# Key sums with stationary values, filled-up matmuls, split first loads and a new stage order in a gated linear-attention and GEGLU kernel

## The chip, the cores and the metric

The kernel runs on one core of one Trainium2 chip. The metric is the device time of one execution of the whole program, in microseconds; of several runs the median counts. On a core five engines work side by side, each through its own queue, in the order in which the program hands it instructions: TensorE (PE, with PEld for its weight loads), VectorE (DVE), ScalarE (ACT), GpSimd (POOL) and SyncE (SP). SP, ACT and POOL also issue DMAs.

## The reference

A block of linear attention and a gated MLP are mixed token by token (S = 2048 tokens, D = 576, 32 heads of 18, DF = 4608):

```
q, k, v = split(x @ wqkv)                      # 32 heads of 18
phi(t)  = where(t > 0, t + 1, exp(t)) + 1e-6
kv  = sum over tokens of phi(k) x v            # per head, 18 x 18
z   = sum over tokens of phi(k)
o   = (phi(q) @ kv) / (phi(q) . z + 1e-6)
a   = o @ wo
b   = (gelu(x @ w_gate) * (x @ w_up)) @ w_down
out = g * a + (1 - g) * b,    g = sigmoid(sum(x * gate_w))
```

## The kernel before

All matmul operands are float32 held as a high and a low part (fp32r tiles with "hi" and "lo"), and a product is taken as hi·hi + hi·lo + lo·hi. `split` makes the parts: ACT copies the high part, DVE (or POOL) subtracts it for the low one. D = 576 is cut into two halves of 128 + 128 + 32 rows; the three 32-row pieces of a half (hi·hi, hi·lo, lo·hi) share one matmul of 96 partitions, so a projection is 14 matmuls.

The program runs through four stages.

**Start and prologue.** `x0` and `raw_of` are the first input tiles and the K|V weights `wkv`, loaded on SP's queue in column and row pieces; `x_split` and `w_part` split them into `xo` (inputs) and `kvw[i]`, i the half. `proj_mm(t, c, ...)` projects token tile t (128 tokens) onto the column part c of `CH` (378, 326 and 450 columns: keys; the rest of the keys, the first values and the gate; the values). The first two token tiles are held open in six PSUM tiles, four of pool `bank` and two of pool `pair`, and their 84 matmuls are handed out by the operands' order of arrival.

**Key stage.** For each of 16 token tiles the projection, then `kv_post` (phi of the keys into `pkh` and `pkl`, values into `vt`), then `kv_state`, two tiles behind: for five groups of heads (126, four times, and 72 columns) it adds phi(k) transposed times [1 1 | v hi | v lo] to PSUM (`acc_a`, `acc_b`), the keys stationary and `vt` moving, once with `pkh` and once with `pkl`. Behind the projections run loads and splits for later stages.

**Mixing stage.** Its order is written out by hand in word lists given to `run(...)`; a word is a letter and hexadecimal arguments, and each word hands its instructions to the engines' queues at once. For a batch b of 512 tokens, a group g of heads, a token tile t of the batch or a third kt of the rows:

- `s` sums out of PSUM (and masked per head), `t` transposes them, `u` splits them, `z` stores the row of key sums to `z_d` and reads it back, `n` makes the den weights `zmk`, `v` the gates
- `w i o f l c`: load of wo, its split, the product `head_out` of a group's kv with wo, its store to `kw_d`, the load of `kwr` in rows of 128 and its split into `KW`
- `Q a h d`: query projection (14 matmuls of 512 columns; 10 for group 4), phi of it into `r`, its split into `hl`, the `den` matmuls
- `r`: reciprocals. The denominators of 32 heads are copied out by ACT, added and inverted by DVE, stored to `rden_d` repeated per row, and read back as `rb` with 128 partitions
- `p m e`: r times `rb`, split (`p`); the mixed product with `KW` (28 matmuls of 288 columns into one `pair`); its scaled copy by ACT and store (`ga`)
- `x` (`keep_x`): three stores of 1280 KB each of `xo` slots that the MLP's second half needs
- `X y Y`: load of a chunk of inputs in another arrangement (`xc`), its sums and differences on DVE, its split by ACT and POOL into the slots S1 to S4 of `xo`
- `W G g`: first weights and first products of the MLP

PSUM holds here three `bank` tiles, two `pair` tiles (of two banks each) and one `den`. `hl` has three buffers, `p` two, `rb` three; `r` of batch 1 takes the tile of batch 2's.

**MLP.** A Strassen-like scheme of seven products a feature block, over 18 blocks, twice; its order is the table `ORDER`.

Of the kernel before, what the change touches and what calls it, by code (L numbers as in the profile page):

```python
# [8 lines left out]
F32 = mybir.dt.float32  # L9
# [18 lines left out]
CW = 126 + NG * 64 + 128  # L28
# [22 lines left out]
def tile_gated_mix(ctx, tc, xt, xs, wkv, wq, wo, wgu, wgt, wdn, cst, out):  # L51
# [8 lines left out]
    rden_d = {(b, h): dram.tile([H, DH, BS // 2], F32, name=f"rden_d{b}{h}") for b in range(NB) for h in range(2)}  # L60
# [95 lines left out]

    KTS = [(i, kt) for i in range(2) for kt in range(3)]
# [22 lines left out]
    CH = [(0, 378), (378, 326), (704, 450)]  # L180
# [46 lines left out]
    def kv_state(t):
        _, ph, pl = pk.pop(t)
        v = vt.pop(t)
        for g in range(NG):  # L230
            w = 2 + 2 * GR[g]
            mv = v[:, g * VW:g * VW + w]
            if g < 4:
                o = acc_a[:GR[g], g // 2, (g % 2) * VW:(g % 2) * VW + w]
            else:
                o = acc_b[:GR[g], 0, :w]
            for i, p in enumerate((ph, pl)):
                nc.tensor.matmul(o, p[:, GO[g]:GO[g] + GR[g]], mv,  # L238
                                 start=(t == 0 and i == 0 and g in (0, 2, 4)),
                                 stop=(t == NST - 1 and i == 1), skip_group_check=True)  # L240
# [3 lines left out]
    for n, (t, c) in enumerate(first):  # L244
        ps_of[t, c] = bank() if n < 4 else pair()[:, 0]
# [155 lines left out]
    rs = [rp.tile([128, NG, BS], F32, name=f"r{i}") for i in range(3)]  # L401
    r_of = {2: rs[0], 3: rs[1], 0: rs[2], 1: rs[0]}
# [63 lines left out]
    wide = acc_a[:126, :, :2 * VW].rearrange("p a (b c) -> p a b c", b=2)  # L466
    last = acc_b[:72, 0]

    def sums_out():
        nc.vector.tensor_copy(zc[:126, :4].rearrange("p (a b) -> p a b", a=2), wide[:, :, :, 0])  # L470
        nc.vector.tensor_copy(zc[:72, 4:5], last[:, 0:1])
# [6 lines left out]
        nc.sync.dma_start(zq[:, :4], at(0, [[1, 128], [128, 4]]))  # L478
        nc.sync.dma_start(zq[:, 4:5], at(512, [[0, 2], [1, 64], [1, 1]]))

    def states_out():
        four = (lambda v: v[:126, :4].rearrange("p (a b) c -> p a b c", a=2))
        low = tp.tile([128, D], F32, name="low")
        kvl, kvl_last = low[:, :504].rearrange("p (g c) -> p g c", g=4), low[:72, 504:]
        nc.scalar.activation(four(kvl), wide[:, :, :, 128:254], AF.Copy)
        nc.scalar.activation(kvl_last, last[:, 74:146], AF.Copy)
        nc.vector.tensor_tensor(four(kvm), wide[:, :, :, 2:128], four(kvl), OP.add)
        nc.vector.tensor_tensor(kvm[:72, 4, :72], last[:, 2:74], kvl_last, OP.add)

        for g in range(NG):  # L490
            R = GR[g]
            nc.vector.tensor_tensor(kvm[:R, g, :R], kvm[:R, g, :R], mask[:R, :R], OP.mult)

    turned = []

    def states_turn():
        tps = pair()
        turned[:] = [tps[:GR[g], g // 4, (g % 4) * 126:(g % 4) * 126 + GR[g]] for g in range(NG)]
        for g in range(NG):
            R = GR[g]  # L500
            nc.tensor.transpose(turned[g], kvm[:R, g, :R], ident[:R, :R])
# [27 lines left out]
    def head_out(g):  # L529
# [3 lines left out]
        kh, kl = kvt[:R, g, 0, :R], kvt[:R, g, 1, :R]  # L533
# [64 lines left out]
    def reciprocals(b):  # L598
        ps = den_of.pop(b)
        for h in range(2):  # L600
# [6 lines left out]
            nc.sync.dma_start(src, bass.AP(tensor=rd.tensor, offset=rd.offset, ap=[list(rd.ap[0]), [0, DH], [1, HB]]))  # L607
        for h in range(2):
            src, rb = rden_d[b, h], rb_of[b, h]
            nc.sync.dma_start(rb[:, :4], bass.AP(  # L610
                tensor=src.tensor, offset=src.offset, ap=[[HB, 128], [128 * HB, 4], [1, HB]]))
            nc.sync.dma_start(rb[:, 4], bass.AP(
                tensor=src.tensor, offset=src.offset + 512 * HB, ap=[[0, 2], [HB, 64], [1, HB]]))
# [12 lines left out]
    def mixed(b, t):  # L626
# [3 lines left out]
        ops += [(p[:, 0, 4], KW[:, 0, 4]), (p[:64, 0, 4], KW[:64, 1, 4])]  # L630
# [45 lines left out]
h11 e31 p32 d10 d11 Y1 p33 m32 h12 d12 a13 e32 p01 m33 W0 h13 h14 e33 p00 X2 y2 d13 m01 d14 r1 m00 Y2  # L676
# [57 lines left out]
G1 G6 G7 g1 p03 G2 e01 m03 p02 g6 e00 g7 e03 m02 p10 m10 e02 p11 m11 W1 p13 e10 p12 e11 g2 m13 e13 m12 e12  # L734
# [356 lines left out]
```

## Time and profile before

| what | value |
|---|---|
| three runs | 1532.23, 1524.12, 1527.63 us; median 1527.63 |
| profiled execution | 1529.19 us; its span from first to last instruction 1527.4; mean granted clock 0.998 |
| busy share of the span | PE 99%, PEld 87%, DVE 72%, POOL 49%, ACT 38% |
| DMA | 293.57 MB in 117884 packets, mean 192 GB/s |
| prologue's matmuls end | 24.24 us |
| key stage's last matmul ends | 146.6 us |
| mixing stage's last mixed product ends | 306.3 us |

The span is shorter than the execution's time because the program's entry and exit lie around it. Busy shares are averages over the whole span; the MLP from 306 us on makes up four fifths of it, so they say little on the stages in front of it, which the change touches. Those are read by stretches.

### The profile page before, as it was taken

The numbers are of one execution on the slowest core, as the hardware profiler recorded it, in microseconds if no ns is written. First come the engines' busy times: TensorE is split into PE (matmuls) and PEld (weight loads), VectorE is DVE, ScalarE is ACT, GpSimd is POOL, SyncE is SP. The second block draws the span as 40 slices with busy tenths as digits, with TensorE's granted clock in tenths as the row PEclk, the third lists the DMA queues.
The fourth block names the chain that finished last, engine by engine and source line by source line (L and its number), as shares of the span: only waits on it lengthen the run. The fifth ranks groups of instructions, "written<-read, shape, count | busy, mean of one in ns | idle before, by whom it ended". The sixth has DMA issues, their size and how long they took to land.

```text
span 1527.4 us, 21407 instructions
## 1 busy us (share of the span) xinstructions
PE 1505.2 (99%) x8179; PEld 1326.5 (87%) x8179; DVE 1106.8 (72%) x1693; ACT 578.8 (38%) x967; POOL 745.2 (49%) x710
## 2 busy tenths in 40 slices
PE   8999999999999999999999999999999999999998
PEld 8999778788888888888888888888888888888887
DVE  6444567578888888888887777777777777777776
ACT  6555655334334333343434323223222222232223
POOL 1474222167878788788776724323233223232323
PEclk9999999999999999999999999999999999999999
DMA  5676666655665667656556475433443344334441
GB/s 202 201 257 224 204 170 218 211 190 200 220 226 205 226 241 261 235 204 222 201 193 225 143 303 206 179 146 137 175 173 136 136 158 175 137 145 184 181 173 62
DMA packets 117884, 293.57 MB, mean 192 GB/s; under 512 B 6806, under 2 KB 88918, under 8 KB 107414
## 3 DMA queue, kind: packets, MB, share of 16 engines
q1 hardware_dynamic: 114258, 279.48, 52.1%
q10 hardware_dynamic: 3236, 10.63, 1.9%
q0 software_dynamic: 288, 2.10, 0.4%
q8 instruction: 64, 1.05, 0.3%
q14 instruction: 38, 0.31, 0.1%
HBM read 177.15 MB, written 115.03 MB: 191 GB/s over the span
## 4 chain that ended last, share of the span: by engine, by line
PE 92%; DMA 3%; POOL 2%; issue 2%; ACT 1%; DVE 1%; SPq 0%; POOLq 0%; DVEq 0%; ACTq 0%
PE bank L694 52%; PE pair L791 25%; PE bank L187 8%; PE pair L633 3%; PE bank L421 1%; PE pair L238 1%; DMA raw<-wo 1%; POOL xo L660 1%; DMA xo<-xop_d 1%; DMA xc<-xs 1%; POOL sums L781 0%; POOL kw L557 0%; PE pair L187 0%; PE pair L993 0%; DMA raw<-wkv 0%
## 5 line engine op out<-in xcount | busy, mean ns | idle before, releaser
L713 DVE TENSOR_TENSOR sums<-pair,sums 128x576 f32<-128x576 f32 x474 | 354.6, 754 | 160.9 <-PE pair L791 149.0
L694 PE MATMUL bank<-xo,wg 128*128 128x512 f32 x1764 | 442.0, 393 | 5.1 <-POOL xo L660 2.4
L694 PE MATMUL bank<-xo,wu 128*128 128x512 f32 x1764 | 430.4, 393 | 0.8 <-DVE p L713 0.8
L694 PEld LDWEIGHTS bank<-xo,wu 128*128 128x128 f32 x1764 | 323.8, 188 | 64.3 <-DVE p L713 1.2
L694 PEld LDWEIGHTS bank<-xo,wg 128*128 128x128 f32 x1764 | 322.5, 188 | 65.6 <-POOL xo L660 3.6
L791 PEld LDWEIGHTS pair<-wd,h 128*128 128x128 f32 x1680 | 248.2, 189 | 17.3
L791 PE MATMUL pair<-wd,h 128*128 128x288 f32 x1680 | 259.2, 296 | 0.0
L791 PEld LDWEIGHTS pair<-wd,hx 128*128 128x128 f32 x1260 | 179.1, 189 | 9.3
L791 PE MATMUL pair<-wd,hx 128*128 128x288 f32 x1260 | 184.4, 295 | 0.0
L707 ACT ACTIVATE p<-bank 128x512 f32<-128x512 f32 x72 | 43.0, 597 | 354.5 <-PE bank L694 348.3
L857 POOL TENSOR_TENSOR wd<-draw,wd 128x432 fp32r<-128x432 f32 x68 | 75.1, 1123 | 191.8 <-ACT wd L707 191.8
L833 POOL TENSOR_TENSOR h<-e,h 128x512 fp32r<-128x512 f32 x70 | 96.4, 1377 | 140.6 <-ACT h L707 140.6
L833 POOL TENSOR_TENSOR hx<-e,hx 128x512 fp32r<-128x512 f32 x70 | 96.6, 1401 | 112.7 <-ACT hx L707 112.7
L707 ACT ACTIVATE h<-e 128x512 fp32r<-128x512 f32 x107 | 67.3, 629 | 211.9 <-DVE e L713 211.9
L849 POOL TENSOR_TENSOR work<-work 128x256 f32<-128x256 f32 x136 | 113.4, 844 | 6.0 <-DMA work<-wgu 0.6
L187 PE MATMUL bank<-kvw,xo 128*128 128x378 f32 (+5 forms) x560 | 106.9, 345 | 5.8 <-ACT kvw L81 5.7
L187 PEld LDWEIGHTS bank<-kvw,xo 128*128 128x128 f32 (+1 forms) x560 | 97.3, 192 | 10.3 <-ACT kvw L81 6.2
L713 DVE TENSOR_TENSOR u<-bank,p 128x512 f32<-128x512 f32 x72 | 49.6, 689 | 47.1 <-PE bank L694 32.3
L707 ACT ACTIVATE hx<-e 128x512 fp32r<-128x512 f32 x105 | 63.9, 626 | 35.2 <-DVE e L713 35.2
L713 DVE TENSOR_TENSOR e<-bank,e 128x512 f32<-128x512 f32 x106 | 72.5, 684 | 1.2
L707 ACT ACTIVATE wd<-draw 128x864 fp32r<-128x864 f32 (+1 forms) x35 | 32.7, 934 | 99.3 <-PE pair L791 99.3
L633 PE MATMUL pair<-kw,p 128*128 128x288 f32 x448 | 66.0, 301 | 0.4 <-POOL kw L557 0.3
(173 smaller groups left out, 1829.1 us busy)
## 6 DMA issues: line engine op xcount, KB each, us to landing
wg<-wp_d SPq DMA_DIRECT2D x17, 2240.0 KB
wu<-wp_d SPq DMA_DIRECT2D x17, 2240.0 KB
wp_d<-wg SPq DMA_DIRECT2D x16, 2240.0 KB
wp_d<-wu SPq DMA_DIRECT2D x16, 2240.0 KB
draw<-wdn SPq DMA_DIRECT2D x35, 576.0 KB
work<-wgu SPq DMA_DIRECT2D x34, 512.0 KB
xo<-xop_d SPq DMA_DIRECT2D x7, 1280.0 KB
wt_d<-tail_op SPq DMA_DIRECT2D x15, 448.0 KB
```

The source lines that it names most:

```text
L187: nc.tensor.matmul(out_t[:, :n], xa, kvw[i][:rows, r, lo:lo + n], start=(k == 0), stop=(k == 13))
L238: nc.tensor.matmul(o, p[:, GO[g]:GO[g] + GR[g]], mv, start=(t == 0 and i == 0 and g in (0, 2, 4)), stop=(t == NST - 1 and i == 1), skip_gr ...
L421: nc.tensor.matmul(ps, qw[i][:rows, c:c + 128], xa, start=(k == 0), stop=(k == 13))
L633: nc.tensor.matmul(y[:, i, :288], pa, w[:, i * 288:(i + 1) * 288], start=(n == 0), stop=(n == 13))
L660: nc.gpsimd.tensor_tensor(xo[rows, S2 + k, lo], raw[rows, k], f32(xo[rows, S2 + k, kt]), OP.subtract)
L694: nc.tensor.matmul(ps, w_, x_, start=start and i == 0, stop=i == 6, skip_group_check=not start)
L707: nc.scalar.activation(o, i, AF.Copy)
L713: nc.vector.tensor_tensor(o, a, b, op)
L791: nc.tensor.matmul(pr[q][:, j, :288], h[:, hl, c], wd[:, b, wl], start=start and i == 0, stop=i == 2, skip_group_check=not start)
L833: op(name + "l", lambda n, e, a=a, f=src_of: e.tensor_tensor(hb[a][:, 1], f(), f32(hb[a][:, 0]), sub))
L849: op(f"{name}T{i + 1}", lambda n, e, o=o, a=a, b=b: e.tensor_tensor(o, a, b, sub))
L857: op(f"dl{x}{j}", lambda n, e, i=i, src=src, c=c: e.tensor_tensor(wd[:, i, 1, c], src[:, :, c], f32(wd[:, i, 0, c]), sub))
```

## The change

Six things change.

1. **First loads.** The K|V weights of the first row block come in three column parts, two on ACT's queue and one on SP's, where all lay on SP's; `w_part` follows the parts. The six open tiles take operands sorted by column part. Seven matmuls of zeros (one zeroed row block of an input slot, into a `pair` tile that the prologue takes over) stand ahead of the first real one.
2. **Key sums.** `kv_state` swaps its operands: the high part of the values, with two columns of ones behind, is stationary (128 columns), and `pk` (hi and lo side by side) moves; the low part of the values is stationary for the high part of the keys only. The sums come out the other way round, so the five transposes (`t`) and the identity in `cst` go, and the row of key sums is one row of 2.3 KB of `kvm`. The mask moves into `u`.
3. **Filled-up matmuls.** The low part of `KW`'s last group is zero in its lower 64 partitions, and the mixed product's last two matmuls run over 128 partitions.
4. **rden.** Stored with 9 repeats of a head, not 18, and read in twelve DMAs a batch instead of four, each row twice.
5. **The word lists** of the mixing stage and of the MLP's first products are new, with `x` in the second list behind `m20`.
6. Memsets on DVE for zeros and ones.

```diff
-CW = 126 + NG * 64 + 128
+CW = 126 + NG * 64
...
-    rden_d = {(b, h): dram.tile([H, DH, BS // 2], F32, name=f"rden_d{b}{h}") ...
+    rden_d = {(b, h): dram.tile([H, DH // 2, BS // 2], F32, name=f"rden_d{b}{h}") ...
...
-    nc.sync.dma_start(raw_of[0, 0][:, :CA], wkv[0, 0, :, :CA])
-    nc.sync.dma_start(x0[0][:, 0:1, :256], xt[0, 0, :, 0:1, :256])
-    nc.sync.dma_start(raw_of[0, 0][:, CA:], wkv[0, 0, :, CA:])
...
+    zero = xo[:, S1, 0]
+    nc.vector.memset(f32(zero), 0.0)
+    warm = pair()
+    for _ in range(7):
+        nc.tensor.matmul(warm[:, 1], zero[:, :128], zero, start=True, stop=True)
...
+    w_first(nc.scalar, 0, *cols[0])
+    w_first(nc.scalar, 0, *cols[2])
+    x_first(nc.sync, 0)
+    w_first(nc.sync, 0, *cols[1])
+    x_first(nc.sync, 1)
+    w_first(nc.sync, 1, 0, KVC)
...
-        for c, e in (((0, CA), (CA, KVC)) if n == 0 else ((0, KVC),)):
+        for c, e in (cols if n == 0 else ((0, 704), (704, KVC)) if n == 1 else ((0, KVC),)):
...
     def kv_state(t):
-        _, ph, pl = pk.pop(t)
+        p = pk.pop(t)[1]
         v = vt.pop(t)
         for g in range(NG):
-            w = 2 + 2 * GR[g]
-            mv = v[:, g * VW:g * VW + w]
-            if g < 4:
-                o = acc_a[:GR[g], g // 2, (g % 2) * VW:(g % 2) * VW + w]
-            else:
-                o = acc_b[:GR[g], 0, :w]
-            for i, p in enumerate((ph, pl)):
-                nc.tensor.matmul(o, p[:, GO[g]:GO[g] + GR[g]], mv,
-                                 start=(t == 0 and i == 0 and g in (0, 2, 4)),
-                                 stop=(t == NST - 1 and i == 1), skip_group_check=True)
+            R, k = GR[g], slice(GO[g], GO[g] + GR[g])
+            o = acc_a[:, g // 2, (g % 2) * 252:(g % 2 + 1) * 252] if g < 4 else acc_b[:, 0, :2 * R]
+            nc.tensor.matmul(o, v[:, g * VW:g * VW + 128], p[:, :, k], start=(t == 0 and g in (0, 2, 4)),
+                             stop=False, skip_group_check=True)
+            nc.tensor.matmul(o[:R, :R], v[:, g * VW + 128:g * VW + 128 + R], p[:, 0, k], start=False,
+                             stop=(t == NST - 1), skip_group_check=True)
...
-        for t, c in first:
+        for t, c in sorted(first, key=lambda a: (a[1], a[0])):
...
+    nc.vector.memset(f32(KW)[64:, 1, 4], 0.0)
...
-        nc.sync.dma_start(at(0, [[1, 126], [126, 4]]), zc[:126, :4])
-        nc.sync.dma_start(at(504, [[1, 72], [1, 1]]), zc[:72, 4:5])
+        nc.sync.dma_start(at(0, [[D, 1], [1, D]]), kvm[126:127])
...
-    def states_turn():
...
     def states_split():
-        for g in range(NG):
-            R = GR[g]
-            split(kvt[:R, g, 0, :R], kvt[:R, g, 1, :R], turned[g])
+        f = kvm[:126, :504].rearrange("p (g c) -> p g c", g=4)
+        nc.vector.tensor_tensor(f, f, bass.AP(tensor=mask.tensor, offset=mask.offset,
+                                              ap=[[mask.ap[0][0], 126], [0, 4], [1, 126]]), OP.mult)
+        nc.vector.tensor_tensor(kvm[:72, 504:], kvm[:72, 504:], mask[:72, :72], OP.mult)
+        split(kvt[:126, 0], kvt[:126, 1], kvm[:126])
...
-w2 Q21 w0 v Q22 s z a21 t i2 i0 Q24 h21 a22 u a24 Q34 a34 w3 o2 Q20 x Q32 Q31 n i3 f2 o3 a20 a32 h20 o0 f3 w4
...
+s Q24 a24 w1 i1 Q20 u z w2 i2 Q21 Q23 a21 o1 a20 h21 o2 w4 i4 f1 w0 i0 Q22 n f2 o4 a23 f4 h20 w3 i3 o0 Q30 f0
...
         for h in range(2):
             src, rb = rden_d[b, h], rb_of[b, h]
-            nc.sync.dma_start(rb[:, :4], bass.AP(...))
-            nc.sync.dma_start(rb[:, 4], bass.AP(...))
+            for g in range(NG):
+                n = min(64, H * DH // 2 - 64 * g)
+                for k in range(64 // n):
+                    nc.sync.dma_start(rb[64 * k:64 * k + 64, g] if n < 64 else rb[:, g], bass.AP(
+                        tensor=src.tensor, offset=src.offset + 64 * g * HB, ap=[[HB, n], [0, 2], [1, HB]]))
...
-        ops += [(p[:, 0, 4], KW[:, 0, 4]), (p[:64, 0, 4], KW[:64, 1, 4])]
+        ops += [(p[:, 0, 4], KW[:, 0, 4]), (p[:, 0, 4], KW[:, 1, 4])]
...
-G1 G6 G7 g1 p03 G2 e01 m03 p02 g6 e00 g7 e03 m02 p10 m10 e02 p11 m11 W1 p13 e10 p12 e11 g2 m13 e13 m12 e12
+G1 G6 g1 G2 p02 e01 p03 e00 G7 g6 m02 e02 m03 g7 p10 m10 e03 p11 m11 W1 p13 e10 p12 e11 m13 g2 e13 m12 e12
```

Three places where instructions move. The first is PE at the program's start. A row is the line, the operation, what it writes and reads, the output's partitions and columns, and how many alike follow; `kvw_160` is the first half of the K|V weights. Before:

```order
L187 MATMUL bank<-kvw_160,xo 128x378 x3
L187 MATMUL bank<-kvw_160,xo 128x326 x3
L187 MATMUL bank<-kvw_160,xo 128x450 x3
L187 MATMUL bank<-kvw_160,xo 128x378 x3
L187 MATMUL pair<-kvw_160,xo 128x326 x3
L187 MATMUL pair<-kvw_160,xo 128x450 x3
```

The same place now:

```order
L165 MATMUL pair<-xo 128x512 x7
L201 MATMUL bank<-kvw_160,xo 128x378 x6
L201 MATMUL bank<-kvw_160,xo 128x326 x3
L201 MATMUL pair<-kvw_160,xo 128x326 x3
L201 MATMUL bank<-kvw_160,xo 128x450 x3
L201 MATMUL pair<-kvw_160,xo 128x450 x3
```

The zeros stand first, and both token tiles take one column part before the next is wanted.

The second place is SP behind the key sums: `raw<-wo` are the loads of wo, `z_d` and `zq` the row of key sums, `xop_d<-xo` the stores of `keep_x`, `kwr` the loads of `kw_d`, `rden_d_70` and `_71` the first batch's two halves. Before:

```order
L519 DMA raw<-wo 128x576 x2
L476 DMA z_d<-zc 126x4x1
L477 DMA z_d<-zc 72x1
L478 DMA zq<-z_d 128x4x1
L479 DMA zq<-z_d 128x1x1
L519 DMA raw<-wo 128x576
L581 DMA xop_d<-xo 128x2560 x3
L519 DMA raw<-wo 128x576 x2
L549 DMA kwr<-kw_d 128x576 x3
L552 DMA kwr<-kw_d 64x576 x2
L607 DMA rden_d_70<-rb 576x1x256
```

Now:

```order
L513 DMA raw<-wo 128x576
L491 DMA z_d<-kvm 1x576
L492 DMA zq<-z_d 128x4x1
L493 DMA zq<-z_d 128x1x1
L513 DMA raw<-wo 128x576 x4
L543 DMA kwr<-kw_d 128x576
L601 DMA rden_d_70<-rb 288x1x256
L601 DMA rden_d_71<-rb 288x1x256
L607 DMA rb<-rden_d_70 128x1x256 x4
L607 DMA rb<-rden_d_70 64x1x256 x2
L607 DMA rb<-rden_d_71 128x1x256 x4
L575 DMA xop_d<-xo 128x2560 x3
```

(Rows between are left out in the second.) The second load of wo stands behind the store and the reads of the key sums, and the three stores behind the first batch's `rb`, with no load of wo after them.

The third place is around `r0`, the reciprocals of batch 0, with the second input chunk (`xc<-xc` is y1, `xo<-xc` is Y1). DVE before, where `r_1677` is the phi tile of batch 1 and `r_1679` that of batch 0:

```order
L567 SCALAR_TENSOR_TENSOR hl<-r_1679,hl 128x512
L650 TENSOR_TENSOR xc<-xc 128x512
L651 TENSOR_TENSOR xc<-xc 128x512
L652 TENSOR_TENSOR xc<-xc 128x512
L653 TENSOR_TENSOR xc<-xc 128x512
L605 TENSOR_TENSOR rb<-rb,den 32x256
L606 RECIPROCAL rb<-rb 32x256
L437 SCALAR_TENSOR_TENSOR r_1677<-bank,r_1677 128x512 x2
```

DVE now, with `r_1676` the phi tile of batch 1 and `r_1677` that of batch 3:

```order
L615 SCALAR_TENSOR_TENSOR r_1677<-r_1677,rb 128x5x128
L617 TENSOR_TENSOR p<-r_1677,p 128x512
L618 TENSOR_TENSOR p<-r_1677,p 64x128
L645 TENSOR_TENSOR xc<-xc 128x512
L646 TENSOR_TENSOR xc<-xc 128x512
L647 TENSOR_TENSOR xc<-xc 128x512
L648 TENSOR_TENSOR xc<-xc 128x512
L599 TENSOR_TENSOR rb<-rb,den 32x256
L600 RECIPROCAL rb<-rb 32x256
L449 SCALAR_TENSOR_TENSOR r_1676<-bank,r_1676 128x512
```

ACT at the same place now (`ga_d_88`, `_90` and `_87` are the stores of e23, e31 and e22):

```order
L633 ACTIVATE ga<-pair,gate 128x576
L635 DMA ga_d_88<-ga 128x576
L616 ACTIVATE p<-r_1677 128x640
L598 ACTIVATE rb<-den 32x256 x2
L447 ACTIVATE r_1676<-bank 128x512
L448 ACTIVATE r_1676<-r_1676 128x512
L633 ACTIVATE ga<-pair,gate 128x576
L635 DMA ga_d_90<-ga 128x576
L635 DMA ga_d_87<-ga 128x576
L652 ACTIVATE xo<-xc 128x4x512
```

On both engines the four `xc<-xc` still stand directly ahead of the first `rb` addition, but a11, e31 and e22 now stand behind the two copies of `den`, and the scaled copy of p30 just ahead of them.

More of the change, by code (lines that the diff above doesn't have):

```diff
@@ L59, in tile_gated_mix @@
     gate = keep.tile([128, 2, NST], F32, name="gate")
-    rden_d = {(b, h): dram.tile([H, DH, BS // 2], F32, name=f"rden_d{b}{h}") for b in range(NB) for h in range(2)}
+    rden_d = {(b, h): dram.tile([H, DH // 2, BS // 2], F32, name=f"rden_d{b}{h}") for b in range(NB) for h in range(2)}
     z_d = dram.tile([D, 1], F32, name="z_d")
@@ L191, in tile_gated_mix @@
     for v in vbuf:
-        nc.vector.memset(f32(v).rearrange("p (g c) -> p g c", g=NG)[:, :, 0:2], 1.0)
+        v = f32(v).rearrange("p (g c) -> p g c", g=NG)
+        nc.vector.memset(v[:, :, 126:128], 1.0)
+        nc.vector.memset(v[:, 4, 72:126], 0.0)
     def kv_post(t, c, ps, part):
         if c == 0:
-            pk[t] = (kp.tile([128, D], F32, name="e"), kp.tile([128, D], F32R, name="pkh"),
-                     kp.tile([128, D], F32R, name="pkl"))
+            pk[t] = (kp.tile([128, D], F32, name="e"), kp.tile([128, 2, D], F32R, name="pk"))
             vt[t] = vbuf[t % 2]
-        r, ph, pl = pk[t]
+        r, (ph, pl) = pk[t][0], (pk[t][1][:, i] for i in range(2))
         v3 = vt[t].rearrange("p (g c) -> p g c", g=NG)
@@ L244, in tile_gated_mix @@
     for n, (t, c) in enumerate(first):
-        ps_of[t, c] = bank() if n < 4 else pair()[:, 0]
+        ps_of[t, c] = bank() if n < 4 else (warm if n == 4 else pair())[:, 0]
     for ops in ((0, 1, 2), (3, 4, 5), (6,), (7, 8, 9)):
-        for t, c in first:
+        for t, c in sorted(first, key=lambda a: (a[1], a[0])):
             proj_mm(t, c, ps_of[t, c], ops)
@@ L453, in tile_gated_mix @@
     cs = tp.tile([128, CW], F32, name="cs")
-    kvm = tp.tile([128, NG, 126], F32, name="kvm")
-    kvt = tp.tile([128, NG, 2, 126], F32R, name="kvt")
-    zc = tp.tile([128, NG], F32, name="zc")
+    kvm = tp.tile([128, D], F32, name="kvm")
+    kvt = tp.tile([128, 2, D], F32R, name="kvt")
     zq = tp.tile([128, NG], F32, name="zq")
     nc.sync.dma_start(cs, cst)
-    mask, sel, ident = cs[:, :126], cs[:, 126:126 + NG * 64], cs[:, 126 + NG * 64:]
+    mask, sel = cs[:, :126], cs[:, 126:]
     def gates():
@@ L464, in gates, with states_out @@
         nc.vector.tensor_scalar(gate[:, 1], gate[:, 0], -1.0, 1.0, op0=OP.mult, op1=OP.add)
-    wide = acc_a[:126, :, :2 * VW].rearrange("p a (b c) -> p a b c", b=2)
-    last = acc_b[:72, 0]
+    def states_out():
+        wide = acc_a[:, :, :504].rearrange("p a (b h c) -> p a b h c", b=2, h=2)
+        four = (lambda v: v[:, :504].rearrange("p (a b c) -> p a b c", a=2, b=2))
+        last = acc_b[:, 0, :144]
+        low = tp.tile([128, D], F32, name="low")
+        nc.scalar.activation(four(low), wide[:, :, :, 1], AF.Copy)
+        nc.scalar.activation(low[:, 504:], last[:, 72:], AF.Copy)
+        nc.vector.tensor_tensor(four(kvm), wide[:, :, :, 0], four(low), OP.add)
+        nc.vector.tensor_tensor(kvm[:, 504:], last[:, :72], low[:, 504:], OP.add)
@@ L479, in sums_out @@
         nc.sync.dma_start(zq[:, 4:5], at(512, [[0, 2], [1, 64], [1, 1]]))
[L481 to L488, printed above, removed]
-        for g in range(NG):
-            R = GR[g]
-            nc.vector.tensor_tensor(kvm[:R, g, :R], kvm[:R, g, :R], mask[:R, :R], OP.mult)
@@ L532, in head_out @@
         y = y_of[g] = pair()
-        kh, kl = kvt[:R, g, 0, :R], kvt[:R, g, 1, :R]
+        kh, kl = (kvt[:R, i, GO[g]:GO[g] + R] for i in range(2))
         for k, (ka, wl) in enumerate(((kh, 0), (kh, 1), (kl, 0))):
@@ L663, in tile_gated_mix @@
     run("""
-r2 h30 c2 Q03 c4 h32 a03 Q33 c3 d30 a33 Q04 h31 d31 d32 h33 a04 p21 l1 h34 X0 Q02 a02 p20 d33 Q01 d34 r3 Q00
-c0 c1 a00 Q14 a01 m21 h00 h01 m20 p23 d00 e20 e21 Q10 y0 p22 m23 m22 d01 Y0 a10 Q12 X1 h04 a14 p31 h02 d02 e22
-Q11 e23 p30 h03 y1 d03 d04 r0 a12 m30 e30 a11 m31 h10 Q13
+h22 d22 c1 Q32 l2 a30 h23 l3 d23 h24 X0 h30 d24 Q31 c4 a33 c2 r2 d30 a32 c0 a31 c3 h32 h31 Q01 a01 Q34 d31 h33
+a34 Q00 p20 d32 Q04 h34 a00 d33 a04 p21 h00 m20 x Q02 y0 h01 d34 m21 Q03 r3 d00 h04 d01 a02 a03 h02 Q10 h03
+d02 Q11 e20 d03 p23 m23 Y0 p22 a10 d04 e21 p31 m22 h10 e23 p30 X1 y1 r0 a11 m31 e31 Q14 e22 m30 Y1 a14 p33 h11
+Q12 a12 d10 Q13 d11 e30 m33 p32 h12 d12 a13
     """)
@@ L675, in tile_gated_mix @@
     run("""
-h11 e31 p32 d10 d11 Y1 p33 m32 h12 d12 a13 e32 p01 m33 W0 h13 h14 e33 p00 X2 y2 d13 m01 d14 r1 m00 Y2
+W0 m32 p01 h13 d13 X2 h14 e33 e32 m01 p00 d14 y2 m00 r1 Y2
     """)
```

42 lines of the change are left out of this document (15 added, 27 removed).

## The prediction

> **What bounds the kernel now.** I read the page first (engine shares, the chain that ended last), then the span cut into stages, then the order in time inside the stages that the change touches.
>
> ```profile
> PE 1505.2 (99%) x8179; PEld 1326.5 (87%) x8179; DVE 1106.8 (72%) x1693; ACT 578.8 (38%) x967; POOL 745.2 (49%) x710
> PE 92%; DMA 3%; POOL 2%; issue 2%; ACT 1%; DVE 1%; SPq 0%; POOLq 0%; DVEq 0%; ACTq 0%
> ```
>
> TensorE bounds: 92% of the chain is its own work. So an edit is worth what it takes off PE's own row, or off a stretch in which PE stands still or runs slow. The stages show where these are (us; PE busy and matmuls; granted clock; DMA share; GB/s):
>
> ```profile
> 0.00:24.20 24.20, 18.39 (x84) 1.00 0.83 287
> 24.20:146.60 122.40, 122.40 (x749) 1.00 0.64 219
> 173.00:180.00 7.00, 5.13 (x21) 0.76 0.43 128
> 193.00:205.00 12.00, 9.96 (x42) 1.00 0.82 237
> 205.00:212.00 7.00, 6.61 (x32) 1.00 0.18 49
> 212.00:269.00 57.00, 56.96 (x345) 1.00 0.64 203
> 269.00:280.40 11.40, 7.83 (x24) 0.85 0.50 114
> 280.40:306.30 25.90, 25.90 (x175) 1.00 0.77 259
> ```
>
> The key stage (24 to 147) and most of the mixing stage are full. The start, and four stretches between 173 and 280, are not. From 306 on the code is the same, so I leave it alone.
>
> **The start: 1.9 us gained.** Seven matmuls of zeros run before the first operands land, and the first loads are split by columns over two queues.
>
> ```profile
> 10.54 2.14 PE L187 MATMUL pair<-kvw,xo 128*128 128x326 f32 x6
> 14.70 1.22 PE L187 MATMUL pair<-kvw,xo 128*128 128x326 f32 x6
> 17.11 1.35 DVE L139 TENSOR_TENSOR kvw<-raw,kvw 32x1154 fp32r<-32x1154 f32 x1
> 24.24 4.68 PE L187 MATMUL bank<-kvw,xo 128*128 128x378 f32 x28
> ```
>
> The same six shapes take 2.14 us at 10.5 and 1.22 at 14.7, so PE runs at half pace until about 12.5, and the prologue's 84 matmuls end at 24.24. (The clock column says 1.00 here; the durations decide.) With PE fast from the outset, the operands limit: the last low part ends on DVE at 17.11 + 1.35 = 18.46, and its time hangs on bytes that have to land before it, which stay the same. Behind it stand some 22 of the last block's 24 matmuls, at (1.22 - 0.16 of drain) / 6 = 0.177: 18.46 + 3.9 = 22.4, so 1.9 earlier. Bounds: 0.5 lost (smaller loads land later, zeros don't speed the clock up) to 2.5 gained.
>
> **The key sums: 0.8 us gained, not 4.8.** Per token tile, ten matmuls of 254 or 146 columns become five of 252 or 144 and five of 126 or 72: 2324 columns fall to 1728. But every matmul loads its own weights, and the load of the next starts as the last one starts streaming:
>
> ```profile
> 35.98 0.28 PE L238 MATMUL pair<-vt,pkl 128*126 128x254 f32 x1
> 36.09 0.23 PE L238 MATMUL pair<-vt,pkh 128*72 128x146 f32 x1
> 36.16 0.23 PE L238 MATMUL pair<-vt,pkl 128*72 128x146 f32 x1
> 36.09 0.14 PEld L238 LDWEIGHTS pair<-vt,pkl 128*72 128x72 f32 x1
> 36.16 0.30 PEld L187 LDWEIGHTS bank<-kvw,xo 128*128 128x128 f32 x2
> ```
>
> Between two 72-wide loads a 146-column matmul has a pitch of 0.07. The same 146 columns ahead of a 128-wide load hold the queue longer: that load starts at 36.16 and the one behind it 0.19 before 36.46, at 36.27, so 0.11. A full-width load sets a floor of 0.11, and a matmul of 126 columns ahead of one costs 0.11, not 126 columns' worth. By that a tile costs 4 x (0.118 + 0.108) + 0.07 + 0.11 = 1.08 after, 8 x 0.119 + 0.07 + 0.11 = 1.13 before: 0.05 x 16 tiles = 0.8. Bounds: if streaming alone counted (0.07 for 146 columns, so 0.06 for 126 and 0.04 for 72) it would be 4.8 gained; if the switch between widths costs something, 0.5 lost. I take the floor, since its row has the same kind of load.
>
> The Trainium skill (TensorE: Matmul & The Clock Gate, section Back-to-back issue gap) gives about 81 ns for each 128-column matmul in a stream of load and matmul pairs. By that figure 80 short matmuls would each cost some 27 ns less than here, 2.2 us, and the estimate of the whole would be 1511.2 instead of 1513.4; the trace's 0.11 speaks against it.
>
> **The 64-partition matmuls: 6.6 us gained.** Each of 16 mixed products ended in two matmuls of 64 partitions; now all 28 have 128, with zeros below.
>
> ```profile
> 285.80 3.49 PEld L633 LDWEIGHTS pair<-kw,p 128*128 128x128 f32 x26 [0.17 <-issue]
> 289.46 0.29 PEld L633 LDWEIGHTS pair<-kw,p 64*128 64x128 f32 x2 [0.17 <-issue]
> 289.91 3.48 PEld L633 LDWEIGHTS pair<-kw,p 128*128 128x128 f32 x26 [0.16 <-issue]
> ```
>
> The load queue stands still before and after the two, where it runs gapless inside the 26. One product's period is 289.91 - 285.80 = 4.11. Twenty-six full ones have a pitch of (3.49 - 0.19) / 25 = 0.132, so 28 would take 3.70: 0.41 x 16 = 6.6. PE is full there, so it counts whole. Bounds: 5 to 7.
>
> **The transposes: 0.5 gained.** Five go, with their split in ten small operations:
>
> ```profile
> 153.11 0.66 PE L501 MATMUL pair<-cs,kvm 126*126 126x126 f32 x5
> ```
>
> 0.66 less its drain. What follows on ACT and DVE (one split of 576 columns, the copies over 128 rows, the small memsets) lies beside the query matmuls, which in the new order come one after another there (Q24, Q20, Q21, Q23, 12 us of PE); without them the 2 us from sums to split would stand bare.
>
> **The new order: waits out 11.3, one wait in 5.3.** In the four slack stretches PE stood still 1.87, 2.04, 0.39 and 3.57 us, 7.9 in all. At clocks of 0.76 and 0.85 it lost 0.24 x 7.00 and 0.15 x 11.40 more, 3.4. Their causes: loads of wo behind the three large stores of `keep_x`, den matmuls behind ACT and DVE, and the last `token_split` with too little PE work ahead of G6 and G7. I followed the new order by hand, engine by engine, adding durations of these rows from the last key sum on. The stores of `keep_x` now stand behind the first batch of `rb`, and no load of wo behind them: o4's low part is ready 15 us after the key sums, PE reaches o4 at 17. Of the den matmuls, d30 comes 5 us after its operand, d33 6. `token_split` of the third chunk gives S2's low part 1 us before G6 needs it, and S3's 1 us before G7, which now stands behind G2. So I take all of it out; bounds: half to all, since the last two have little to spare.
>
> On SP the load of the second wo tile (w2) now stands behind the store of the sums and its two reads.
>
> ```profile
> SPq L478 <- DMA z_d<-zc: 6.5, 1, 6.5
> ```
>
> The reads waited 6.5 us for a store of 4-byte pieces; now it is one row of 2.3 KB. If it took 6.5 again, w2 would land about 4 us late, ACT would stand at i2 and PE some 3 us at o2 and Q22: in the range, not in the sum, since one row is nearest to the loads of whole rows.
>
> What is late next: the second input chunk. In the new order its sums (y1) stand on DVE ahead of the den additions of r0, and ACT's second copy of `den` waits for the first of these; behind that copy stand a11, e31 and e22, and m30 needs e22's pair of banks.
>
> ```profile
> 222.15 1.90 ACT L657 ACTIVATE xo<-xc 128x2048 fp32r<-128x2048 f32 x1
> 224.13 5.48 POOL L660 TENSOR_TENSOR xo<-xc,xo 128x512 fp32r<-128x512 f32 x4 [12.29 <-ACT xo L657]
> xc<-xs POOLq DMA_DIRECT2D x1, 1024.0 KB, 5.5
> 216.98 0.69 DVE L650 TENSOR_TENSOR xc<-xc 128x512 f32<-128x512 f32 x1
> 185.27 0.40 DVE L605 TENSOR_TENSOR rb<-rb,den 32x256 f32<-32x256 f32 x1
> 185.76 0.38 ACT L604 ACTIVATE rb<-den 32x256 f32<-32x256 f32 x1 [0.73 <-DVE rb L605]
> 190.19 0.60 ACT L435 ACTIVATE r<-bank 128x512 f32<-128x512 f32 x1
> 219.16 0.74 ACT L638 ACTIVATE ga<-pair,gate 128x576 f32<-128x576 f32 x1 [3.25 <-PE pair L633]
> 190.79 0.63 PE L576 MATMUL den<-hl,zmk 128*128 128x512 f32 x2
> 191.26 2.49 PE L424 MATMUL bank<-xo,qw 128*128 128x512 f32 x10
> 195.34 3.39 PE L421 MATMUL bank<-xo,qw 128*128 128x512 f32 x14
> ```
>
> From the end of Q03: a03 and h02, h03 on ACT 4 x 0.6, e20 with its store 1.1, p23 behind DVE's scaling 1.6: 5.1. Then the split 1.9, POOL's four 5.5 and 0.4 to the issue, the load 5.5, y1 4 x 0.7; then the add 0.4, the copy 0.4, a11 1.2, e31 and e22 1.9 with a store between, 4.1 with the gaps: 25.3. PE has between them Q10, Q11 (3.25 each), Q14 (2.33), m23, m22, m31 (3.70 each) and nine den matmuls (0.23 each): 22.0. So m30 waits 3.3 or a little more, 3.4. The stretch at 269 shows that an idle time of this size drops the clock (0.85, 1.7 us there): 1.9 more. Bounds: 0 to 7.
>
> The Trainium skill (TensorE: Matmul & The Clock Gate, Part 1) says that the clock falls only after an idle window of about 3.4 us; by that rule a wait just under it would leave the clock alone, and the estimate would be 1511.5. The trace differs: 1.87 us of idle in 7.00 went with a clock of 0.76, so I keep the loss.
>
> **The sum.** The profiled execution took 1529.19 (span 1527.4), 0.1% above the median 1527.63. 1529.2 - 1.9 - 0.8 - 6.6 - 0.5 - 11.3 + 5.3 = 1513.4. A difference under 0.5%, 7.6 us, can't be told from none.
>
> **Rivals.**
> No new wait: if the chunk lands earlier or ACT is ahead, 1513.4 - 5.3 = 1508.1, with streaming-bound key sums 1504. For it: 3.4 is a small difference of two sums of 20 and more. Against: every term of the chain is a row.
> The order trades waits: other late operands cost half of the 11.3 again, 1519. For it: ACT and DVE run in order, and much is moved. Against: in the walk only m30 waits.
> Slower: the loads of `rb` come in 12 parts a batch instead of 4, and each waits for its turn on SP.
>
> ```profile
> 187.47 2.63 SPq L607 DMA_DIRECT2D rden_d<-rb x2
> 192.28 0.38 SPq L610 DMA_DIRECT2D rb<-rden_d x1
> 200.79 0.83 DVE L620 SCALAR_TENSOR_TENSOR r<-r,rb 128x640 f32<-128x640 f32 x1 [2.80 <-DMA rb<-rden_d]
> ```
>
> First store to first use is now 13.3 us. In the new order PE has 16.3 us of work for the first batch, less 2.8 and 2.7 of work at its ends: 10.8. Halved stores win back some 2.5; eight more issues cost 8 x 0.38 = 3.0. If loads followed each other singly, six of 2 us a half, each of four batches would come some 6 us late: 4 x 6 + 2 = 26 more, 1539. It decides from 5.9 us a batch. Against: eight may be under way at once, and the later batches have 8 us to spare.
> Nothing to measure: if zeros, floor and order bring nothing and only the 64-partition term comes, 1522.6. For it: the start's gain and the waits rest on operands in time. Against: four stretches have four causes.
>
> **Chances.** Forecast 0.50 (1509 to 1517); no new wait 0.27; traded waits 0.14; slower 0.04; nothing 0.05. Faster by over 0.5% takes the first two and half of the third: 0.84; same 0.12; slower 0.04. The range 1504 to 1520 takes in the first two and most of the third.
>
> **What would show it.** Right: six pairs at full pace from the first operand, prologue's end near 22.4; 126-column matmuls 0.11 apart; 28 loads without a gap, 3.7 a product; PE full from 147 on but for one wait of 3 to 4 us before m30, released by ACT, with a clock dip. Wrong: short matmuls 0.06 apart, that wait absent, or waits at m20 for `rb`.

## The result and the profile after

The changed kernel takes 1515.95 us (median of 5 runs, 1514.99 to 1517.35) against 1529.01 before (5 runs): a ratio of 0.9916, 95% interval 0.9898 to 0.9935. It is faster by 13.1 us; forecast were 1513.4 and 15.8 less. The profiled execution took 1517.35 with a span of 1515.6 and is the slowest of the five.

The experiments below come from three later sets of rounds. There the kernel before had medians of 1527.67 to 1528.05, and after was not timed again, so a difference between after and an experiment is uncertain by one or two us.

The span of after cut into stretches (TensorE alone: length, busy time and matmuls, granted clock, DMA share, GB/s):

```profile
0.00:22.30 22.30, 19.22 (x92) 1.00 0.80 279
144.30:227.00 82.70, 82.70 (x432) 1.00 0.56 179
227.00:240.00 13.00, 9.93 (x44) 0.74 0.51 148
260.00:272.00 12.00, 8.40 (x35) 0.86 0.47 130
272.00:295.40 23.40, 23.40 (x174) 1.00 0.69 232
```

From the key sums to 227 PE is full, where before had three slack stretches (173, 193, 205). Two slack stretches are left, 227 to 240 and 260 to 272, with 3.07 and 3.60 us of idle time and lowered clocks. The first was forecast, the second not. The landmarks of PE's row in after are the starts of the first matmul behind the prologue, behind the key stage and behind the last mixed product:

```profile
22.29 1.02 PE L201 MATMUL bank<-kvw,xo 128*128 128x378 f32 x5
144.31 0.94 PE L436 MATMUL bank<-xo,qw 128*128 128x512 f32 x3
295.23 3.38 PE L690 MATMUL bank<-xo,wg 128*128 128x512 f32 x14
```

The same landmarks in before:

```profile
24.24 4.68 PE L187 MATMUL bank<-kvw,xo 128*128 128x378 f32 x28
146.61 1.13 PE L421 MATMUL bank<-xo,qw 128*128 128x512 f32 x4
306.34 3.56 PE L694 MATMUL bank<-xo,wg 128*128 128x512 f32 x14
```

So the prologue brought 24.24 - 22.29 = 1.95, the key stage 146.61 - 144.31 - 1.95 = 0.35, the mixing stage 306.34 - 295.23 - 2.30 = 8.8, and the rest of the span's 11.8 (0.7) lies in the unchanged code behind. The first of these differences varies between profiles: in the four kernels with the old start this landmark lies at 22.98 to 24.24, in the ten with the new loads at 21.70 to 23.06, on the mean 1.7 earlier. The second doesn't: the key stage takes 122.3 to 122.5 us with the old key sums and 121.9 to 122.1 with the new ones.

### The profile page after: what moved, and what is told of

It reads as the page before. It is cut to its first block, busy times and chain, and to the rows that moved or that the text cites. A ratio compares the mean times of both kernels' runs of the same rounds, so it can differ in the third digit from the quotient of the medians.

```text
span 1515.6 us, 21450 instructions
## 1 busy us (share of the span) xinstructions
PE 1497.4 (99%) x8181; PEld 1326.2 (88%) x8181; DVE 1107.5 (73%) x1690; ACT 577.6 (38%) x965; POOL 746.9 (49%) x710
## 4 chain that ended last, share of the span: by engine, by line
PE 93%; DMA 2%; DVE 1%; issue 1%; POOL 1%; ACT 1%; POOLq 0%; SPq 0%; DVEq 0%; ACTq 0%
PE bank L690 53%; PE pair L787 26%; PE bank L201 7%; PE pair L628 2%; PE bank L433 2%; PE pair L248 1%; DMA xo<-xop_d 1%; DMA raw<-wkv 1%; POOL xo L655 1%; DMA xc<-xs 0%; PE pair L989 0%; POOL sums L777 0%; PE bank L436 0%; PE pair L250 0%; PE den L570 0%
```

## Experiments

Each was timed four to eleven times beside the kernel before; ratios are to it, with a 95% interval. What was expected stands ahead of each result.

**The filled-up matmuls alone**, on before:

```diff
+    nc.vector.memset(f32(KW)[64:, 1, 4], 0.0)
...
-        ops += [(p[:, 0, 4], KW[:, 0, 4]), (p[:64, 0, 4], KW[:64, 1, 4])]
+        ops += [(p[:, 0, 4], KW[:, 0, 4]), (p[:, 0, 4], KW[:, 1, 4])]
```

> Before, with only the zeros in KW and the last two matmuls of each mixed product over 128 partitions. Theory: each of 16 products falls from 4.11 to about 3.70 us (28 loads without a gap) on a PE that is full there, so 6.0 to 6.6 us less than before. Rival: the gap of the load queue is paid elsewhere (the product is bound by its operands from ACT and DVE, or the next stretch waits that much longer), then 3 us or less.

Measured: 1527.46 against 1527.67, ratio 0.9999 (0.9989 to 1.0008). The rival holds: nothing is left. What PE waited for in this run between 240 and 280 (who waits, for whom: us in total, times, longest):

```profile
PE bank L695 <- POOL xo L661: 2.7, 2, 2.4
PE bank L695 <- DMA wg<-wp_d: 2.6, 1, 2.6
```

The last stretch of these (TensorE alone):

```profile
262.00:280.00 18.00, 11.64 (x32) 0.71 0.47 108
```

And in order of time the issue of the third chunk's load and its first use:

```profile
251.12 0.57 POOL L647 DMA_DIRECT2D xc<-xs  x1 [0.31 <-POOL xo L661]
264.94 0.69 DVE L651 TENSOR_TENSOR xc<-xc 128x512 f32<-128x512 f32 x1 [7.28 <-DMA xc<-xs]
```

PE came to G1 some 7 us earlier than in before and met the first MLP weights (`wg`) still under way beside the chunk: 13.8 us passed from the chunk's issue to its first use, where before has 10.4 (257.44 to 267.8). On top, the clock of 0.71 over 18.00 us is 5.2 us of missing clock, where before missed 0.15 x 11.40 = 1.7 at this place. Load, sums, split by ACT and POOL, next load is a ring through one buffer, `xc`; in before PE waited 2.4 us for the same split of POOL, so there too the ring, and not PE, ended last.

**The filled-up matmuls undone where the ring does not end last** (the base is the kernel "both waits" below):

> The kernel of the run before in this call, with the last two matmuls of each mixed product over 64 partitions again. In the old order the filled-up matmuls alone brought 0.2 us. Theory: there the chain of the input chunks (load, sums, split, next load) ended last, and gave back what PE won; with g1 free of the chunk, PE ends last and the term counts: 5 to 6.6 us more than its base. Rival: the chain of the chunks still ends last, or the 64-partition matmuls cost less than the period says: less than 2 us more.

Measured: 1514.28 against 1509.77, 4.5 us (ratios 0.9914, 0.9901 to 0.9928, and 0.9886, 0.9872 to 0.9899). Now the term counts. A product of this run with another operation behind it, and one of after:

```profile
214.62 4.06 PE L628 MATMUL pair<-kw,p 128*128 128x288 f32 x28
214.23 3.87 PE L628 MATMUL pair<-kw,p 128*128 128x288 f32 x28
```

The next operation starts at 218.61 here and at 217.94 in after, so the product's period is 3.99 and 3.71. Only where a product follows directly is it 4.11 here: six times of sixteen, so the price is 10 x 0.28 + 6 x 0.39 = 5.1, not 6.6. The den matmuls at 243 to 246 wait 1.0 us here and 2.1 in the base, so 1.1 of the 5.1 went to them.

**The new word lists alone**, on before (`z t u` in place of `u z`, since the transposes remain):

> Before, with only the new word lists (the transposes stand behind the row of key sums and ahead of the split). Theory: the new order takes out the waits at 174, 193 to 205 and 272 to 280, and puts in two, before m30 and before G2, with a drop of the clock each; net 1 to 4 us less than before. Rival 1 (the prediction's sum, 11.3 out and 5.3 in): 6 us less. Rival 2: the old store of key sums in pieces of 4 bytes stands ahead of the second load of wo in the new order, so o2 waits some 3 us and the order alone brings nothing or costs up to 2.

Measured: 1534.0 against 1527.67, ratio 1.0041 (1.0028 to 1.0054): slower by 6.3, worse than rival 2. Its three longest waits on PE in the mixing stage:

```profile
PE pair L536 <- ACT wos L525: 6.1, 1, 6.1
PE bank L695 <- ACT p L708: 3.0, 1, 3.0
PE pair L633 <- ACT ga L638: 1.7, 1, 1.7
```

The first is `head_out` of group 2 behind the second load of wo, which now stands behind the store of key sums. The other two are the forecast ones, before G2 and before m30.

**The key sums undone** in after, all else kept (lists with `z t u`):

> After, with the key sums of before (keys stationary, transposes behind the row of key sums, that row stored in pieces of 4 bytes) under the new word lists and everything else of the change. Theory: the swap is worth little on PE (0.4 us of key sums, 0.5 of transposes), but its row of 2.3 KB lets the second load of wo start; undone, o2 waits some 7 us as it did with the order alone: 6 to 9 us more than after, 1522 to 1525. Rival (the prediction's terms): 0.8 and 0.5, so 1517 to 1517.5.

Measured: 1528.20, ratio 0.9999 (0.9988 to 1.0011): without the new key sums the whole gain is gone, 12.2 us by the medians. SP's wait for the store of the row, and PE's for what follows:

```profile
SPq L493 <- DMA z_d<-zc: 6.2, 1, 6.2
PE pair L551 <- ACT wos L540: 5.8, 1, 5.8
```

The stretch (length, then busy time and instructions of PE, PEld, DVE, ACT and POOL, then clock, DMA share, GB/s):

```profile
158.00:170.00 12.00, 5.54 (x18) 4.30 (x17) 4.07 (x7) 5.65 (x10) 3.18 (x3) 0.72 0.38 96
```

SP's wait at the same place in after:

```profile
SPq L492 <- DMA z_d<-kvm: 0.9, 1, 0.9
```

PE stands still 12.00 - 5.54 = 6.5 us there. The clock of 0.72 over 12 us is 3.4 us of missing clock, of which some 0.9 fell into the standing still (the trace has half clock from 163.1 on, PE starts again at 164.28): 6.5 + 2.5 = 9.0 of the 12.2. In after the read waits 0.9 for one row of 2.3 KB.

**The same with `w2` ahead of `z`:**

```diff
-s Q24 a24 w1 i1 Q20 z t u w2 i2 Q21
+s Q24 a24 w1 w2 i1 Q20 z t u i2 Q21
```

> The kernel of the run before, with the load w2 ahead of the store of the row of key sums. Theory: o2's wait is that store's; with the load ahead, what is left of the swap are 0.9 us of PE and the ten small splits behind the transposes: 1 to 3 us more than after, 1517 to 1519. Rival: o2 waits for the splits or for the chunks' chain, not for the load: within 2 us of the run before.

Measured: 1524.28, ratio 0.9978 (0.9969 to 0.9986): a third of the 12.2 comes back. Neither case holds wholly. o2 no longer waits, but the next loads of wo stand behind the same reads: ACT waits 6.1 us for one, and PE 2.7 behind the copy that follows it on ACT:

```profile
ACT wos L540 <- DMA raw<-wo: 6.1, 1, 6.1
PE pair L551 <- ACT ko L558: 2.7, 1, 2.7
```

**g1 apart.** After, with the copy g1 in a free tile, for the first block:

```diff
-            copy(p1, first[1])
+            first["c"] = hp.tile([128, BS], F32, name="qt", bufs=1)
+            copy(first["c"], first[1])
...
-            tt(u2, first[6], p1, add)
+            tt(u2, first[6], first["c"], add)
```

> After, with the copy g1 written to an unused tile in place of p1, for the first block alone. Theory: p1 lies on the memory of the input chunk xc, so ACT's copy waits until POOL has read the chunk to the end, and G2, which needs the copied bank, waits 3.8 us for that, with 1.5 of lowered clock behind it; freed of that, 4 to 5.5 us less than after. Rival: G2 or G7 waits for the low parts that POOL makes anyway (S3's comes 4.4 us after the split begins), so the wait only moves to G7 and less than 1.5 us are gained.

Measured: 1511.42, ratio 0.9894 (0.9879 to 0.9908), 4.5 less than after by the medians; the intervals overlap a little, so the rows decide. Those in after, where ACT's copy into `p1` waits for POOL to finish with `xc`:

```profile
261.56 5.78 POOL L655 TENSOR_TENSOR xo<-xc,xo 32x512 fp32r<-32x512 f32 x4 [19.82 <-ACT xo L652]
267.37 0.60 ACT L703 ACTIVATE p<-bank 128x512 f32<-128x512 f32 x1 [5.90 <-POOL xo L655]
268.02 4.98 PE L690 MATMUL bank<-xo,wg 128*128 128x512 f32 x14 [3.60 <-ACT p L703]
```

and in this run, where the 28 products run through:

```profile
259.61 6.61 PE L690 MATMUL bank<-xo,wg 128*128 128x512 f32 x28
261.42 0.60 ACT L703 ACTIVATE qt<-bank 128x512 f32<-128x512 f32 x1 [1.37 <-PE bank L690]
```

The copy reads no chunk; only its target's memory, freed with the pool of `xc`, ties it to POOL.

**y1 later**, in after: `X1 y1 r0 a11 m31` becomes `X1 r0 a11 y1 m31`.

> After, with the word y1 moved behind r0 and a11, so that DVE's additions of the denominators don't wait for the second input chunk. Theory: the wait of 3.2 us before m30 hangs on the chunk through y1, the additions, ACT's second den copy, a11, e31 and e22; without it m30 starts on time, and with the clock's drop gone 4 to 6 us less than after. Rival: ACT is that far behind by itself, or the later chunk sums hold up Q13 or p33 instead: less than 2 us.

Measured: 1515.96, as after (ratio 0.9926, 0.9913 to 0.9939). The cause is confirmed, the gain is not: the wait before m30 is gone. The den matmuls of batch 1 wait instead, 1.2 us for ACT and 0.9 for DVE, and behind G2's wait the clock stays low for longer than in after (there these 14 matmuls take 4.98, here 6.19):

```profile
PE den L570 <- ACT hl L559: 1.2, 1, 1.2
264.91 6.19 PE L690 MATMUL bank<-xo,wg 128*128 128x512 f32 x14 [3.61 <-ACT p L703]
```

**Both waits**: g1 apart, and `X1 r0 a11 y1 m31 e31 Q14 e22 m30 h11 Y1 p33 a14`.

> After, with g1's copy apart from p1 and, in the word lists, r0 and a11 ahead of y1, h11 and p33 ahead of a14. Theory: both waits of after are gone (before m30 and before G2), and the den matmuls of batch 1, which waited 2.6 us when only y1 was moved, have their operands in time: 4 to 6 us less than with g1 apart alone, 1505.5 to 1507.5. Rival: the second chunk's sums now come later on DVE, POOL's split with them, and the third chunk's load; the products G6 and G7 wait for that instead: within 2 us of g1 apart alone (1509.5 to 1512).

Measured: 1509.77, ratio 0.9886 (0.9872 to 0.9899). It has the lowest median here; but beyond g1 apart it brings 1.7, as its rival said, and the intervals of the two overlap. m30 starts on time, the clock stays at 1.00 through the stage, and two den matmuls wait at 243 and 245 (1.4 and 0.7 us) for h12.

**h12 ahead of p32**, a14 behind d12, on top:

> The kernel with g1 apart and r0, a11 ahead of y1, now with h12 ahead of p32 and a14 behind d12. Theory: the last two waits of the den matmuls (1.6 and 1.0 us at 243 and 245, for h12 behind a14, whose DVE work stood behind p33 slowed by POOL) are gone: 1.5 to 2.6 us less, 1507 to 1508.3. Rival: a14's later end, or p32 behind h12, makes m32 or d14 wait instead: 1509 or more.

Measured: 1512.3, ratio 0.9899 (0.9882 to 0.9916): the rival. d12 is on time; h13 now stands on ACT behind a14, a13 and p01:

```profile
PE den L570 <- ACT hl L559: 2.7, 1, 2.7
```

**The old form of `rden`** in after (18 repeats, four loads a batch):

> After, with the reciprocals repeated 18 times per head in the store and read back in four loads a batch, as before. Theory: first store to first use (10.0 us in after against 13.3 in before) grows by some 3 us, but the first use has 3 us or more to spare in the new order, and so has SP: within 1 us of after. Rival 1: m20 waits for it: 2 to 4 us more than after. Rival 2 (the slower case of the prediction): twelve loads hold up SP, and the old form is 2 us or more faster.

Measured: 1520.38, ratio 0.9951 (0.9937 to 0.9964), 4.4 more than after by the medians; the span of the profiled execution is 2.8 longer (1518.4 against 1515.6). Rival 1 holds. First store to first use takes 190.87 - 177.93 = 12.9 in this run:

```profile
177.93 2.63 SPq L601 DMA_DIRECT2D rden_d<-rb  x2
190.87 0.82 DVE L614 SCALAR_TENSOR_TENSOR r<-r,rb 128x640 f32<-128x640 f32 x1 [2.90 <-DMA rb<-rden_d]
```

In after it is 188.33 - 178.36 = 10.0, with no wait:

```profile
178.36 2.64 SPq L601 DMA_DIRECT2D rden_d<-rb  x2
188.33 0.81 DVE L615 SCALAR_TENSOR_TENSOR r<-r,rb 128x640 f32<-128x640 f32 x1
```

And PE's waits in this run's mixing stage:

```profile
PE pair L627 <- ACT p L615: 1.0, 1, 1.0
PE pair L627 <- ACT ga L632: 4.2, 2, 3.9
```

m20 waits 1.0, and m30 longer than in after (3.9 against 3.1). The twelve loads don't hold up SP in after: they are issued within 7.68 us, one behind the other.

```profile
181.63 7.68 SPq L607 DMA_DIRECT2D rb<-rden_d  x12
```

Whether the halved stores or the smaller loads bring the gain was not tried apart.

**No zeros**, in after:

> After, without the seven matmuls of zeros. Theory: PE runs at half pace until 10 to 12.5 us, as in before, so the prologue's matmuls end 0.7 to 2 us later than 22.1, of which the waits for operands (0.6, 0.3 and 0.7 us) hide a part; the whole 0.5 to 2 us more than after. Rival: the loads over two queues set the prologue's end, and without the zeros it moves by less than 0.3 us.

Measured: 1517.09, ratio 0.9934 (0.9921 to 0.9946), 1.1 more than after, not told apart by the intervals. So the rival holds. PE's first nine real matmuls take 3.07 us without zeros and 1.99 with them, but the prologue's last ones come no earlier with the zeros. This run:

```profile
5.07 3.07 PE L199 MATMUL bank<-kvw,xo 128*128 128x378 f32 x9 [5.07 <-ACT kvw L81]
21.70 1.55 PE L199 MATMUL bank<-kvw,xo 128*128 128x378 f32 x8
```

After (its last ones stand at 22.29 above):

```profile
4.62 1.99 PE L201 MATMUL bank<-kvw,xo 128*128 128x378 f32 x9
8.91 0.61 PE L201 MATMUL bank<-kvw,xo 128*128 128x378 f32 x2 [0.63 <-ACT kvw L81]
```

The time that the zeros save, PE then spends waiting for operands; without them it doesn't wait there.

**The old start**, in after (loads on SP alone, old pieces and order, no zeros):

> After, with the first loads, their splits and the order of the first matmuls as before, and no zeros. Theory: the prologue's matmuls end at 22.8 to 24, as they do in before and its variants, against 21.5 to 22.9 with the new start: 0.7 to 2 us more than after. Rival: the waits before m30 and G2 hang on loads and chunks, not on the start, and swallow it: less than 0.5 us.

Measured: 1519.55, ratio 0.9940 (0.9925 to 0.9955), 3.6 more than after by the medians; the intervals overlap. Its prologue's matmuls end at 23.93, in after at 22.29, and 21.70, the earliest of all, is the run without zeros. So loads and order, not zeros, carry the start, and its worth is nearer to the 1.6 between these ends than to 3.6: the trace of this run also has a lowered clock at 900 us (0.86 over 12 us, where after has 1.00), in code that didn't change.

## Why the prediction was right, and where a step was off

The time lies in the range, at the slow end of the forecast: 13.1 us less by the medians, where the sum gave 15.8 less than the profiled execution. One term of the sum, the waits of the new order, came out at half, and two gains were smaller than forecast. By its steps:

- *The start, 1.9.* The two profiles have 1.95, and the mean of all kernels 1.7. The reason was half wrong: PE does run at full pace earlier with the zeros, but they alone change nothing that shows in the time. "The operands limit" is what held.
- *Key sums, 0.8 and not 4.8.* The stage gained 0.35. The price of a pair of matmuls was right: weight loads start 0.11 apart.

```profile
50.87 0.19 PEld L248 LDWEIGHTS pair<-pk,vt 128*128 128x128 f32 x1
50.98 0.19 PEld L250 LDWEIGHTS pair<-pk,vt 128*126 128x126 f32 x1
50.70 0.33 PE L248 MATMUL pair<-pk,vt 128*128 128x252 f32 x1
50.87 0.22 PE L250 MATMUL pair<-pk,vt 128*126 128x126 f32 x1
50.93 0.33 PE L248 MATMUL pair<-pk,vt 128*128 128x252 f32 x1
```

The short matmul does pass in 0.06, as the sign named for "wrong" had it; its neighbour takes 0.17, and a pair 0.23. The sign was badly chosen: the pair's pitch decides. A tile's ten matmuls take 1.02 in after and took 1.08 (not 1.13) before; the saving of 0.06 a tile shows only in part in the stage's length. The Trainium skill (TensorE: Matmul & The Clock Gate, section LDWEIGHTS (loading the stationary operand)) gives a load's time as its columns divided by 1.2, 107 ns for 128; the 0.11 here agrees.
- *64-partition matmuls, 6.6.* The mechanism shows, 28 loads without a gap:

```profile
191.57 3.88 PEld L628 LDWEIGHTS pair<-kw,p 128*128 128x128 f32 x28
```

The size was too high: 4.11 is the period of a product that another one follows directly. The rest took 4.00, so the term is 5.1 to 5.4, not 6.6. And what it is worth depends on what ends last: 0.2 alone in the old order, 4.5 with the waits gone.
- *The wait before m30, 3.4 and 1.9 of clock.* It came, by the chain that was worked out: chunk, y1, addition, den copy, a11, ga.

```profile
225.59 0.69 DVE L645 TENSOR_TENSOR xc<-xc 128x512 f32<-128x512 f32 x1 [1.71 <-DMA xc<-xs]
228.81 0.38 ACT L598 ACTIVATE rb<-den 32x256 f32<-32x256 f32 x1 [5.58 <-DVE rb L599]
231.15 6.65 PE L628 MATMUL pair<-kw,p 128*128 128x288 f32 x28 [3.07 <-ACT ga L633]
```

PE stood still for 3.07, and m30's 28 matmuls took 6.65 where the same product takes 3.87 on time: 2.8 of clock, more than the 1.9. That price is not fixed: the same wait cost less in other runs, and in one nothing (last section). Taking the wait away alone brought nothing.
- *All four slack stretches out, 11.3.* This is the step that failed. The first three stretches went. The fourth, 3.57 + 0.15 x 11.40 = 5.3 before, did not, though the step said "I take all of it out", since S2's and S3's low parts would come 1 us early. No product waited for those (with g1 apart all 28 run through); but g1 stands ahead of G2 and writes where POOL still reads, which the walk along operands did not see. PE waits 3.60, and G2's 14 matmuls take 4.98 where G1's took 3.38: 5.2 again. That is what the rival "the order trades waits" named, half of the 11.3, by another cause than late operands.

The mixing stage should have given 6.6 + 0.5 + 11.3 - 5.3 = 13.1, and gave 8.8. The products' new period makes 5.4 of it (eight of sixteen took 4.11 before), the transposes 0.5, and 2.9 are left for the new order, where 11.3 - 5.3 = 6.0 was forecast. Idle time and lowered clock as the profile lists them hardly fell, from 11.3 to 3.07 + 2.8 + 3.60 + 1.6 = 11.1. But these sums leave out short gaps and the drain of the last matmul ahead of each gap; counted from start to start, against the usual pitch of each kind of matmul in these runs, the stage's losses fell from some 14.8 to 11.3 (an estimate).
- *The slower rival, `rb` in twelve parts.* Against it the prediction set the halved stores. The new form won: the old one costs 2.8 to 4.4. The twelve loads were issued some 0.64 us apart, not one every 2 us, which no run here shows. The term was left out of the sum because the slack seemed to hide it.
- *The store of key sums.* "If it took 6.5 again ... PE some 3 us": undone with the swap, it costs 12.2, 9.0 of it at this place. The choice (one row is fast) was right, and the lists depend on it; the price was too low, since all later loads of wo stand behind that read.

The parts do not add up. Undone one by one they cost 12.2 (keys), 4.4 (`rden`) and 3.6 (start); lists alone lose 6.3, filling alone wins nothing.

## What to carry to other kernels

Before a saving on the busiest engine is summed, find the ring of loads and buffers that it will catch up with: here a term read from that engine's own row was worth nothing while another chain ended last. In a walk through a new order, follow the memory too: a tile that takes over a freed tile's place waits for its last reader. In an operand swap, look at the layout of what comes out; a row in one partition was worth more here than the columns saved.

## What the runs showed of the hardware

In the rows looked at, VectorE slowed down beside GpSimd's split only where both inputs lay in SBUF. In the "both waits" run POOL works from 234.15 to 239.69; the low part of `p` (0.69 elsewhere) takes 1.27, while an addition with one input in PSUM keeps its 0.68:

```profile
234.15 5.54 POOL L655 TENSOR_TENSOR xo<-xc,xo 128x512 fp32r<-128x512 f32 x4 [13.40 <-ACT xo L652]
234.72 1.27 DVE L617 TENSOR_TENSOR p<-r,p 128x512 fp32r<-128x512 f32 x1 [1.27 <-ACT p L616]
237.32 0.68 DVE L446 TENSOR_TENSOR qt<-qt,bank 64x512 f32<-64x512 f32 x1
```

The Trainium skill (GPSIMD Engine Reference, section Specifications) names this contention for two SBUF inputs; the trace agrees. Whether it is why h11 and h12 came late in two runs was not tried.

The price of a wait in clock was not the same from run to run. m30 behind its wait took 6.65 in after (row above); here are the runs with g1 apart and with `w2` ahead of `z`:

```profile
230.91 5.47 PE L628 MATMUL pair<-kw,p 128*128 128x288 f32 x28 [3.10 <-ACT ga L633]
239.28 3.98 PE L649 MATMUL pair<-kw,p 128*128 128x288 f32 x28 [3.33 <-ACT ga L654]
```

The longest idle time of the three, 3.33, cost no clock: the product takes 3.87 to 3.89 with no wait ahead of it. In all fourteen traces the clock that the profile records is either full or half, and each spell of half clock between the prologue and the program's end lasted 3.41 us or two or three times that: in after 0.26 x 13.00 x 2 = 6.8 at m30 and 0.14 x 12.00 x 2 = 3.4 at G2. Waits of 1.4 and 0.7 us within 3 us left the clock at 1.00, while before had 3.4 us of half clock behind 1.87 in two pieces, and the wait of 2.7 for h13 was followed by 3.4 as well. So the length of a wait alone does not tell its price, and a difference of 2 or 3 us between two profiles can be clock alone. What decides no run settles.
